# Linear attention, slot mixture and MLP in one kernel: products of the middle chunk with the states placed in the off-diagonal quarters of TensorE, beside the first link of the state chain

## The chip, the cores and the metric

The kernel runs on one core of a Trainium2 chip. The metric is the device time of one execution in microseconds (us), the median of several runs. The engines are TensorE (PE, and PEld for its weight loads), VectorE (DVE), ScalarE (ACT), GpSimd (POOL) and SyncE (SP), whose queue issues nearly all DMAs. Each engine takes its instructions in the order in which they are written; semaphores order them across engines.

## The reference

Three stages follow each other. The first is a gated linear attention over 4 batches, 8 heads, 768 steps and 48 features:

```python
for t in range(S):
    state = alpha[:, :, t, :, None] * state + np.einsum('bhd,bhe->bhde', k[:, :, t], v[:, :, t])
    y[:, :, t] = np.einsum('bhd,bhde->bhe', q[:, :, t], state)
```

The second takes its output as 3072 tokens of 384 features into a soft mixture of 8 experts with 4 slots each: logits `x @ phi`, a softmax over tokens that gathers the slots, two matrix products per expert (`w1`, `w2`), and a softmax over slots that gives them back. The third is a gated MLP (`w_gate`, `w_val`, `w_out`) from 384 over 1536 to 384 features. All is computed to float32 accuracy.

## The kernel before

The attention is worked off in a loop of 32 steps (`fast`, L622). Step g is half a sequence (3 chunks of 128 time steps) of one unit n, that is of two heads s = 0 and 1, which lie on partitions 0 to 47 and 64 to 111. Eight steps are one batch. Within a half, three kinds of product make y:

- S = k^T q per chunk and head (`emit_s`, L353), masked to its triangle by DVE (L360) for head 0, and by an ACT copy (L362) and a POOL select (L363) for head 1; then masked S with v (`emit_ip`, L432);
- the state before the chunk with q (`emit_past`, L420), which all chunks have but the first of a sequence;
- the chain of states: k^T v of each chunk (`emit_dh`, L390), to which a link adds the state before by a product with an identity (`emit_st`, L402); ACT scales the sum into the next state (L404).

A float32 product appears as two MATMUL records. L402 and L420 use 64 rows by 64 columns of the array: head 0 the upper left quarter, head 1 the lower right. L353 uses 64 rows by 128 columns, L390 and L432 128 rows by 64 columns, and the transposes of k (`emit_kt`, L371) and of y (`emit_xt`, L462) and the logits (`emit_l`, L453) have shapes of their own.

The order on every engine is that of the code; the loop is a software pipeline written by hand. Step g issues, for PE: the first link of g, S of g+1, the second link, the transposes of k of g+1 and of x = y of g-1, the logits of g-1, now and then a piece of the softmax slots (`pend`), the past products of g, dh of g+1, and the masked products of g. ACT copies the sum of the past and the masked products to x (L434) at the end of the step. DVE runs the two scans over alpha (L307, L314) for step g+3, POOL scales k and q by them (L325) for step g+2.

Beside this, the MLP's weights are turned to float32: `wgv` comes as 64-bit words in 24 loads of 384 KB, one issued by `pump_gv` at the end of a step into one of two buffers. Each takes an ACT pass (`conv_y`, L249) and three DVE passes (`conv(0)`, `conv(1)`, `conv(2)`: L253, L257, L261), spread over one step. `conv_y` stands in ACT's order right after the first link's ACT work; a condition (L627) keeps it out of steps 0 and 1, and out of two steps of each eight after the first eight.

PSUM: PE's products for kt, dh, xt and the slot pieces come from one rotating pool of three banks (`psm`, L179); y has one bank (`ps_y`), in which a past product opens the accumulation and the masked ones close it.

SP issues per step the loads of v (for g+4), of k and q (for g+5) and of alpha (for g+6) as their buffers come free, then one `wgv` load and by a credit (`RATE`) the blocks of `w1`, `w2` and `wo`. After the loop follow the slot softmax of the last batch, the experts (L856, L914) and, from about 190 us to the end, the MLP (L1010, L1011, L1049).

Of the kernel before, what the change touches and what calls it, by code (L numbers as in the profile page):

```python
# [8 lines left out]
F32 = mybir.dt.float32  # L9
# [9 lines left out]
CH = 128  # L19
# [3 lines left out]
NU = H // 2  # L23
NE, NSL, FE = 8, 32, 1024
# [9 lines left out]
LAST = 4  # L34
GV0, RATE = 1, 840
TINY = 2.0 ** -55
NEAR, ROUND = 31600, 19184
LA = 3
# [54 lines left out]
def attention_slots_mlp(ctx: ExitStack, tc: tile.TileContext, kq, at, vt, phi, w1, w2, wgv, wo, cst, out):  # L93
    nc = tc.nc
# [11 lines left out]
    negm = cs[:, 288:289]  # L106
    phs = const.tile([112, NU, NSL], F32, name="phs")
    tots = const.tile([112, B * NU, NC], F32, name="tots")
# [32 lines left out]
    def program(general):  # L141
# [15 lines left out]

        zn = {nm: [0] * n for nm, n in (("a", 4), ("p", 5), ("v", 4), ("w", 2), ("x", 2))}
        zsize = {"a": HW, "p": HB, "v": 288, "w": HW, "x": 384}
        for z in "a0 a1 p2 a2 p3 v0 w0 a3 p4 v1 w1 p0 v2 p1 v3 x0 x1".split():  # L160
            zn[z[0]][int(z[1])] = ar.alloc(zsize[z[0]], 1)
# [10 lines left out]
        def view(r, rows=128):  # L172
            o = r[0] % FAR
            return (near_t if r[0] < FAR else far_t)[0:rows, o:o + r[1]]
# [3 lines left out]

        def psm():  # L179
            return ps_m.tile([128, 512], F32, tag="m", name="m")  # L180

# [195 lines left out]
        def new_g():  # L377
            ng[0] += 1
            return gsts[:, ng[0] % 7, :]

        def emit_dh(g):
            n, h = sgs[g]
            vv[g] = have.pop(("v", g))
            v = view(vv[g]).rearrange("p (c e) -> p c e", e=96)
            t = ktok.pop(g)
            dps[g] = psm()
            for c in range(nk(g)):
                for s in range(2):
                    m = 64 if s == 0 else 48
                    nc.tensor.matmul(dps[g][64 * s:64 * s + m, c * 48:c * 48 + 48], lhsT=t[:, c, 64 * s:64 * s + m], rhs=v[:, c, 48 * s:48 * s + 48], start=(c == 0), stop=True, skip_group_check=True)  # L390

        dps = {}

# [13 lines left out]

        yps = {}


        def emit_past(g):
            n, h = sgs[g]
            q = view(qp[g], 112)
            yps[g] = ps_y.tile([128, 512], F32, tag="y", name="y")
            for c in range(3):
                cc = 3 * h + c
                o = slice(c * CH, (c + 1) * CH)
                for s in range(2) if cc else ():
                    p = slice(0, 64) if s == 0 else slice(64, 112)
                    nc.tensor.matmul(yps[g][p, o], lhsT=gst[n, cc][p, 0:p.stop - p.start], rhs=q[p, o], start=(cc == max(1, 3 * h)), stop=False, skip_group_check=True)  # L420
            del qp[g]
            release(pair.pop(g), z_p, g + 5)

        def emit_ip(g):
            n, h = sgs[g]
            v = view(vv[g]).rearrange("p (c e) -> p c e", e=96)
            ps = yps[g]
            for c in range(3):
                o = slice(c * CH, (c + 1) * CH)
                for s in range(2):  # L430
                    p = slice(0, 64) if s == 0 else slice(64, 112)
                    nc.tensor.matmul(ps[p, o], lhsT=v[:, c, 48 * s:48 * s + p.stop - p.start], rhs=smk[g, s][:, c], start=False, stop=True, skip_group_check=True)  # L432
            xt[g] = (z_x.pop(0), 384)
            nc.scalar.copy(view(xt[g], 112), ps[0:112, 0:384])  # L434
            del smk[g, 0], smk[g, 1], yps[g]
            release(vv.pop(g), z_v, g + 4)

# [7 lines left out]
        def emit_l(g):  # L445
            n, h = sgs[g]
            b, u = units[n]
            if u == 0 and h == 0:
                lps[b] = ps_l.tile([128, 512], F32, tag="l", name="l")
            x = view(xt[g], 112)  # L450
            for j in range(3):
                t0 = j * CH
                nc.tensor.matmul(lps[b][32 * j:32 * j + 32, CH * h:CH * h + CH], lhsT=phs[:, u, :], rhs=x[:, t0:t0 + CH], start=(u == 0 and h == 0), stop=(u == NU - 1), skip_group_check=True)  # L453

        def emit_xt(g, between=lambda: None):
            n, h = sgs[g]
            b, u = units[n]
            x = view(xt[g], 112)
            ps = psm()
            for c in range(3):  # L460
                t0 = c * CH
                nc.tensor.transpose(ps[:, c * 112:(c + 1) * 112], x[:, t0:t0 + CH], ident[0:112, 0:112])  # L462
            between()
            src = bass.AP(ps.tensor, ps.offset, [list(ps.ap[0]), [112, 3], [64, 2], [1, 48]])
            dst = xtok[:, n % 5, 3 * h:3 * h + 3].rearrange("p c (s e) -> p c s e", s=2)
            nc.scalar.copy(dst, src)

        def slot_steps(b):
# [27 lines left out]
            def e_tok():  # L496
# [4 lines left out]
                nc.vector.tensor_copy(st["et"].rearrange("p r e -> p (r e)"), ps[:, 0:192])  # L501

            def part(between=lambda: None):
                ps = psm()
                o = NU * b % 5
                pieces = [(0, o, min(NU, 5 - o))] + [(5 - o, 0, NU - 5 + o)] * (o > 1)
                for r in range(2):
                    if r:
                        between()
                    for u, p, w in pieces:  # L510
                        for j in range(3):
                            nc.tensor.matmul(ps[32 * j:32 * j + 32, 96 * u:96 * u + 96 * w], lhsT=st["et"][:, r, 32 * j:32 * j + 32], rhs=xtok[:, p:p + w, 3 * r + j, :], start=(r == 0 and u == 0), stop=(r == 1), skip_group_check=True)
                if own:
# [62 lines left out]

        def fast():
            pump_units(4)

# [42 lines left out]
            for g in range(NSG):  # L622
                n, h = sgs[g]
                nxt = g + 1 < NSG

                emit_st(g, 1 - h)
                if GV0 < g and (g <= 8 or g % 8 not in (3, 4)):  # L627
                    conv_y()
                if g + 3 < NSG:
# [21 lines left out]
                if g:  # L651
                    emit_l(g - 1)
                    release(xt.pop(g - 1), z_x, g + 1)
                    p = sgs[g - 1][0]
                    if sgs[g - 1][1] == 1 and units[p][1] == NU - 1:
                        pend += slot_steps(units[p][0])
                        late = True
                        pend.pop(0)()
                if pend and not late:
                    pend.pop(0)()  # L660
                emit_past(g)
                if nxt:
# [14 lines left out]
                while credit[0] > 0:  # L677
                    c = credit[0]
                    pump(1)
                    if credit[0] == c:  # L680
                        break
                pump_units()
            for r in z_t:
                drop(r)
# [448 lines left out]
def _arrays(q, k, v, alpha, moe_phi, moe_w1, moe_w2, moe2_w_gate, moe2_w_val, moe2_w_out):  # L1133
# [16 lines left out]
    vt = c(v.reshape(B, NU, 2, NC, CH, D).transpose(0, 1, 4, 3, 2, 5)).reshape(B, NU, CH, NC * 96)  # L1150
    ph = np.zeros((112, NU, NSL), np.float32)
    pr = moe_phi.reshape(NU, 2, D, NSL)
    for s in range(2):
        ph[64 * s:64 * s + 48] = pr[:, s].transpose(1, 0, 2)
    w1 = moe_w1.reshape(2, 4, 3, 128, 2, 512).transpose(0, 4, 2, 1, 3, 5).reshape(2, 2, 4, 3, 128, 512)
# [31 lines left out]
```

## Time and profile before

| | us |
|---|---|
| median of 3 runs | 388.98 (387.81 to 390.64) |
| the profiled execution, own time | 387.89 |
| its span, first to last instruction | 386.2 |
| PE, DVE, ACT, POOL busy over the span | 368.8, 292.4, 200.8, 102.4 |

The page and the views name a line of the code, an engine, an operation, and its tiles as out<-in. In a timeline row the first number is the start from the span's beginning, the second the length; neighbouring instructions of one kind are merged ("x12"), and the idle time before, with what ended it, stands in brackets. A matmul's record is longer than the time that it holds the array, since records overlap; what a group costs is read from start to start. In a windows row stand, for a stretch, its length, then for each engine its busy time and instructions, TensorE's granted clock, the busy share of the DMA engines and their GB/s.

### The profile page before, as it was taken

The numbers are of one execution on the slowest core, as the hardware profiler recorded it, in microseconds if no ns is written. First come the engines' busy times: TensorE is split into PE (matmuls) and PEld (weight loads), VectorE is DVE, ScalarE is ACT, GpSimd is POOL, SyncE is SP. The second block draws the span as 40 slices with busy tenths as digits, with TensorE's granted clock in tenths as the row PEclk, the third lists the DMA queues.
The fourth block names the chain that finished last, engine by engine and source line by source line (L and its number), as shares of the span: only waits on it lengthen the run. The fifth ranks groups of instructions, "written<-read, shape, count | busy, mean of one in ns | idle before, by whom it ended". The sixth has DMA issues, their size and how long they took to land.

```text
span 386.2 us, 8613 instructions
## 1 busy us (share of the span) xinstructions
PE 368.8 (95%) x3308; PEld 277.0 (72%) x3309; DVE 292.4 (76%) x566; ACT 200.8 (52%) x468; POOL 102.4 (27%) x105
## 2 busy tenths in 40 slices
PE   7799999999999999999899999999999999999992
PEld 3577777776777776433478778888888888888781
DVE  6999899999999973306789977777677867977540
ACT  2366665665567455523467655455445446446441
POOL 3379666795587650011200000000000000000000
PEclk9999999999999999999999999999999999999997
DMA  8999999999899986899900013204204104112002
GB/s 276 354 300 343 374 342 316 321 342 338 281 369 361 304 286 217 345 367 413 351 2 0 3 48 111 68 28 126 74 1 153 50 23 153 38 36 82 3 2 90
DMA packets 28627, 74.25 MB, mean 192 GB/s; under 512 B 3216, under 2 KB 11648, under 8 KB 28576
## 3 DMA queue, kind: packets, MB, share of 16 engines
q1 hardware_dynamic: 28256, 73.27, 53.9%
q8 instruction: 28, 0.46, 0.5%
q10 hardware_dynamic: 272, 0.21, 0.2%
q14 instruction: 23, 0.19, 0.2%
q0 software_dynamic: 48, 0.13, 0.1%
HBM read 68.87 MB, written 4.72 MB: 191 GB/s over the span
## 4 chain that ended last, share of the span: by engine, by line
PE 73%; DVE 6%; DMA 3%; ACT 2%; issue 1%; DVEq 0%; ACTq 0%
PE m L1049 22%; PE acc L1049 11%; PE s L353 4%; PE y L432 4%; PE y L420 4%; PE s L1010 4%; PE s L1011 4%; DMA near<-w 3%; PE s L856 3%; PE m L402 3%; PE m L390 2%; PE m L371 2%; PE l L453 2%; PE m L462 2%; DVE near L1016 2%; DVE rnd L1024 1%
## 5 line engine op out<-in xcount | busy, mean ns | idle before, releaser
L1049 PE MATMUL m<-rnd 128*128 128x512 f32 x432 | 129.3, 389 | 0.0
L1049 PEld LDWEIGHTS m<-rnd 128*128 128x128 f32 x432 | 81.1, 188 | 16.8
L1013 ACT ACTIVATE near<-s 128x512 f32<-128x512 f32 x72 | 43.1, 598 | 79.1 <-PE s L1010 79.1
L1049 PE MATMUL acc<-rnd 128*128 128x512 f32 x216 | 81.1, 392 | 0.8 <-DVE rnd L905 0.8
L325 POOL TENSOR_TENSOR far<-far 112x384 f32<-112x384 f32 x61 | 74.5, 1239 | 9.7 <-DVE far L307 4.7
L1016 DVE TENSOR_TENSOR near<-near,s 128x512 f32<-128x512 f32 x72 | 49.3, 685 | 35.3 <-ACT near L1013 35.3
L1024 DVE TENSOR_TENSOR rnd<-near,rnd 128x512 fp32r<-128x512 f32 x72 | 49.4, 686 | 3.1 <-ACT rnd L1022 3.1
L1049 PEld LDWEIGHTS acc<-rnd 128*128 128x128 f32 x216 | 40.5, 188 | 10.2 <-DVE rnd L905 1.6
L1022 ACT CAST rnd<-near 128x512 fp32r<-128x512 f32 x72 | 44.2, 614 | 0.2 <-DVE near L1016 0.2
L404 ACT ACTIVATE far<-m,tots 112x48 f32<-112x48 f32 x80 | 24.2, 302 | 24.1 <-PE m L402 13.3
L307 DVE TENSOR_TENSOR_SCAN far<-far,r 112x388 f32<-112x388 f32 x32 | 30.8, 961 | 5.8 <-DMA far<-at 3.2
L353 PE MATMUL s<-far 64*128 64x128 f32 x384 | 30.5, 289 | 3.5 <-POOL far L325 3.5
L1120 DVE TENSOR_REDUCE amm<-near 112x1 f32<-112x768 f32 x32 | 30.3, 946 | 3.5 <-DMA near<-at 3.5
L363 POOL TENSOR_SCALAR_AFFINE_SELECT far<-far 128x384 f32<-128x384 f32 x32 | 21.7, 677 | 42.3 <-ACT far L362 42.3
L314 DVE TENSOR_TENSOR_SCAN far<-far,r 112x387 f32<-112x387 f32 x32 | 30.7, 959 | 1.1
L434 ACT COPY far<-y 112x384 f32<-112x384 f32 x32 | 15.3, 479 | 27.7 <-PE y L432 27.7
L353 PEld LDWEIGHTS s<-far 64*128 64x128 f32 x384 | 24.4, 187 | 6.1 <-POOL far L325 4.4
L432 PE MATMUL y<-far 128*48 128x128 f32 (+1 forms) x384 | 28.6, 274 | 0.0
L1010 PE MATMUL s<-rnd 128*128 128x512 f32 x72 | 28.3, 393 | 0.0
L1011 PE MATMUL s<-rnd 128*128 128x512 f32 x72 | 28.2, 391 | 0.0
L257 DVE SCALAR_TENSOR_TENSOR near<-near 128x384 uint32<-128x384 uint32 x36 | 21.3, 593 | 8.5 <-ACT near L249 7.6
L261 DVE SCALAR_TENSOR_TENSOR near<-near 128x384 uint32<-128x384 uint32 x36 | 24.5, 681 | 0.3
(163 smaller groups left out, 489.7 us busy)
## 6 DMA issues: line engine op xcount, KB each, us to landing
near<-w SPq DMA_DIRECT2D x18, 768.0 KB, 7.7
far<-kq SPq DMA_DIRECT2D x32, 384.0 KB, 5.3
far<-w SPq DMA_DIRECT2D x14, 768.0 KB, 5.6
near<-wgv SPq DMA_DIRECT2D x24, 384.0 KB, 5.9
far<-at SPq DMA_DIRECT2D x32, 194.0 KB, 5.2
near<-at SPq DMA_DIRECT2D x16, 339.1 KB, 3.4
far<-vt SPq DMA_DIRECT2D x32, 144.0 KB, 4.7
near<-wo SPq DMA_DIRECT2D x12, 384.0 KB, 7.9
```

The costliest lines, as they stand in the source:

```text
L307: nc.vector.tensor_tensor_scan(w[:, ::-1], a[:, ::-1], rst[:, ::-1], 0.0, ALU.mult, ALU.add)
L314: nc.vector.tensor_tensor_scan(a, a, rst[:, 0:387], 0.0, ALU.mult, ALU.add)
L325: eng.tensor_tensor(out=xv, in0=xv, in1=sv, op=ALU.mult)
L353: nc.tensor.matmul(sps[g][s][:, o:o + CH], lhsT=k[64 * s:64 * s + 64, t0:t0 + CH], rhs=q[64 * s:64 * s + 64, t0:t0 + CH], start=True, stop ...
L432: nc.tensor.matmul(ps[p, o], lhsT=v[:, c, 48 * s:48 * s + p.stop - p.start], rhs=smk[g, s][:, c], start=False, stop=True, skip_group_check ...
L1010: nc.tensor.matmul(pg, lhsT=swk[n][:, 128 * o:128 * o + 128], rhs=ctT[t % 4], start=True, stop=True)
L1011: nc.tensor.matmul(pv, lhsT=swk[n][:, 256 + 128 * o:256 + 128 * o + 128], rhs=ctT[t % 4], start=True, stop=True)
L1013: nc.scalar.activation(sg, pg, AF.Silu)
L1016: nc.vector.tensor_tensor(out=h_, in0=sg, in1=pv, op=ALU.mult)
L1022: nc.scalar.copy(hi, h_)
L1024: nc.vector.tensor_tensor(out=lo, in0=h_, in1=hi, op=ALU.subtract)
L1049: nc.tensor.matmul(p, lhsT=passes[j][0][:, sl], rhs=passes[j][1], start=(f == 0 and j == 0), stop=(f == NF - 1 and j == 2))
```

## The change

The past products of step g-1 move from the end of their step into step g, right behind its first link. The masked products now come first and open the accumulation, the past products close it, and the copy to x moves with them. The middle chunk (c = 1) is computed with its two heads swapped: head 0's columns go to partitions 64 and up and head 1's to 0 to 63, so that its past products use the two other quarters of the array, and it has a PSUM bank of its own. So x is copied in two pieces (128 and 256 columns). What reads x undoes the swap: `phs` is held twice, the second time with the heads exchanged, and the gather of slots reads the middle chunk's columns in the other order (`x_rows`). The three rotating banks are allocated once: bank 0 for dh and the links, bank 1 for the middle chunk, kt and the slot pieces, bank 2 for xt. One of the two x buffers goes, `far` shrinks by 128 columns for the larger `phs`, and `conv_y` starts in step 1 in place of step 2, behind the two copies.

```diff
-GV0, RATE = 1, 840
+RATE = 840
-NEAR, ROUND = 31600, 19184
+NEAR, ROUND = 31600, 19056
...
-    phs = const.tile([112, NU, NSL], F32, name="phs")
+    phs = const.tile([112, 2, NU, NSL], F32, name="phs")
...
-        def psm():
-            return ps_m.tile([128, 512], F32, tag="m", name="m")
+        mb = []
+
+        def psm(i=1):
+            return mb[i] if mb else ps_m.tile([128, 512], F32, tag="m", name="m")
...
-            dps[g] = psm()
+            dps[g] = mb[0]
...
+        def swap(c):
+            return int(c == 1 and not general)
+
+        def half(s):
+            return slice(0, 64) if s == 0 else slice(64, 112)
+
+        def y_out(g, s, c):
+            return yps[g][c == 1][half(s ^ swap(c)), CH * (c // 2):CH * (c // 2) + CH]
+
+        def emit_ip(g):
+            yps[g] = ps_y.tile([128, 512], F32, tag="y", name="y"), mb[1]
+            v = view(vv[g])
+            for c in (0, 2, 1):
+                for s in range(2):
+                    o = y_out(g, s, c)
+                    e = 96 * c + 48 * s
+                    nc.tensor.matmul(o, lhsT=v[:, e:e + o.shape[0]], rhs=smk[g, s][:, c], start=(c < 2), stop=True, skip_group_check=True)
+            del smk[g, 0], smk[g, 1]
+            release(vv.pop(g), z_v, g + 4)
 
         def emit_past(g):
             n, h = sgs[g]
             q = view(qp[g], 112)
-            yps[g] = ps_y.tile([128, 512], F32, tag="y", name="y")
             for c in range(3):
                 cc = 3 * h + c
-                o = slice(c * CH, (c + 1) * CH)
                 for s in range(2) if cc else ():
-                    p = slice(0, 64) if s == 0 else slice(64, 112)
-                    nc.tensor.matmul(yps[g][p, o], lhsT=gst[n, cc][p, 0:p.stop - p.start], rhs=q[p, o], start=(cc == max(1, 3 * h)), stop=False, skip_group_check=True)
+                    o = y_out(g, s, c)
+                    nc.tensor.matmul(o, lhsT=gst[n, cc][half(s), 0:o.shape[0]], rhs=q[half(s), c * CH:(c + 1) * CH], start=False, stop=True, skip_group_check=True)
+            xt[g] = (z_x.pop(0), 384)
+            x = view(xt[g], 112)
+            y, z = yps.pop(g)
+            nc.scalar.copy(x[:, CH:2 * CH], z[0:112, 0:CH])
+            nc.scalar.copy(x.rearrange("p (c t) -> p c t", t=CH)[:, 0::2], y[0:112, 0:2 * CH].rearrange("p (c t) -> p c t", t=CH))
             del qp[g]
             release(pair.pop(g), z_p, g + 5)
...
         def emit_l(g):
...
-                nc.tensor.matmul(lps[b][32 * j:32 * j + 32, CH * h:CH * h + CH], lhsT=phs[:, u, :], rhs=x[:, t0:t0 + CH], start=(u == 0 and h == 0), stop=(u == NU - 1), skip_group_check=True)
+                nc.tensor.matmul(lps[b][32 * j:32 * j + 32, CH * h:CH * h + CH], lhsT=phs[:, swap(j), u, :], rhs=x[:, t0:t0 + CH], start=(u == 0 and h == 0), stop=(u == NU - 1), skip_group_check=True)
...
-            ps = psm()
+            ps = psm(2)
...
                 emit_st(g, 1 - h)
-                if GV0 < g and (g <= 8 or g % 8 not in (3, 4)):
-                    conv_y()
+                if g:
+                    emit_past(g - 1)
+                    if g <= 8 or g % 8 not in (3, 4):
+                        conv_y()
...
-                emit_past(g)
...
+            emit_past(NSG - 1)
+            mb.clear()
```

On PE the place is from the logits of a step over its past products to the next ones. Before, in step 2 (l logits, y past products with the bank's number, m dh):

```order
L453 MATMUL l_266<-far_94,phs_73 32x128 x3
L420 MATMUL y_270<-far_94 64x128
L420 MATMUL y_270<-far_94 48x128
L420 MATMUL y_270<-far_94 64x128
L420 MATMUL y_270<-far_94 48x128
L420 MATMUL y_270<-far_94 64x128
L420 MATMUL y_270<-far_94 48x128
L390 MATMUL m_277<-far_94 64x48
```

Now, at the start of the next step (L405 the link, L441 the past products of the step before, m_96 the middle chunk's bank, L356 the S products):

```order
L405 MATMUL m_95<-far_94,cs_72 64x48
L405 MATMUL m_95<-far_94,cs_72 48x48
L441 MATMUL y_279<-far_94 64x128
L441 MATMUL y_279<-far_94 48x128
L441 MATMUL m_96<-far_94 48x128
L441 MATMUL m_96<-far_94 64x128
L441 MATMUL y_279<-far_94 64x128
L441 MATMUL y_279<-far_94 48x128
L356 MATMUL s_310<-far_94 128x128
```

The six past products left their place between the logits and dh and stand behind the link, the middle pair with its column counts exchanged.

On ACT the place is step 3, from the link's ACT work (L404) to the copy of S. Before, L434 being the copy to x:

```order
L434 COPY far<-y 112x384
L404 ACTIVATE far<-m,tots 112x48
L249 ACTIVATE near<-near 128x384
L404 ACTIVATE far<-m,tots 112x48
L374 COPY far<-m 128x336
L466 COPY far<-m 128x288
L362 COPY far<-s 128x384
```

Now, with the same work under L407, L445 and L446 (the copies to x), L252, L377, L478 and L365:

```order
L407 ACTIVATE far<-m,tots 112x48
L445 COPY far<-m 112x128
L446 COPY far<-y 112x2x128
L252 ACTIVATE near<-near 128x384
L407 ACTIVATE far<-m,tots 112x48
L377 COPY far<-m 128x336
L478 COPY far<-m 128x288
L365 COPY far<-s 128x384
```

The one copy ahead of the link's ACT work became two behind it, still ahead of `conv_y`.

On DVE the place is the work of step 1 (scans of step 4, mask of step 2). Before, up to the next step's start:

```order
L306 MEMSET r 112x4
L307 SCALAR_TENSOR_TENSOR far<-far,r 112x388
L309 TENSOR_TENSOR tots<-far,r 112x3
L310 RECIPROCAL r<-tots 112x3
L314 SCALAR_TENSOR_TENSOR far<-far,r 112x387
L360 TENSOR_TENSOR far<-s,cs 128x384
```

Now, the same step with the first conversion in it (L256, L260, L264):

```order
L309 MEMSET r 112x4
L310 SCALAR_TENSOR_TENSOR far<-far,r 112x388
L256 TENSOR_SCALAR near<-near 128x384
L312 TENSOR_TENSOR tots<-far,r 112x3
L313 RECIPROCAL r<-tots 112x3
L317 SCALAR_TENSOR_TENSOR far<-far,r 112x387
L260 SCALAR_TENSOR_TENSOR near<-near 128x384
L363 TENSOR_TENSOR far<-s,cs 128x384
L264 SCALAR_TENSOR_TENSOR near<-near 128x384
```

Every conversion up to step 10 moved one step ahead. On SP the order of the loads is the same up to there; so a `wgv` load, issued at the end of the same step as before, stands one step nearer to the conversion that reads it. The load of k and q waits for the past products in addition, which free its buffer later than before.

More of the change, by code (lines that the diff above doesn't have):

```diff
@@ L156, in program @@
         z_c = [(ar.alloc(GP, 0), GP)]
-        zn = {nm: [0] * n for nm, n in (("a", 4), ("p", 5), ("v", 4), ("w", 2), ("x", 2))}
+        zn = {nm: [0] * n for nm, n in (("a", 4), ("p", 5), ("v", 4), ("w", 2), ("x", 1))}
         zsize = {"a": HW, "p": HB, "v": 288, "w": HW, "x": 384}
-        for z in "a0 a1 p2 a2 p3 v0 w0 a3 p4 v1 w1 p0 v2 p1 v3 x0 x1".split():
+        for z in "a0 a1 p2 a2 p3 v0 w0 a3 p4 v1 w1 p0 v2 p1 v3 x0".split():
             zn[z[0]][int(z[1])] = ar.alloc(zsize[z[0]], 1)
@@ L379, in new_g @@
             return gsts[:, ng[0] % 7, :]
+        dps, yps = {}, {}
         def emit_dh(g):
@@ L390, in emit_dh @@
                     nc.tensor.matmul(dps[g][64 * s:64 * s + m, c * 48:c * 48 + 48], lhsT=t[:, c, 64 * s:64 * s + m], rhs=v[:, c, 48 * s:48 * s + 48], start=(c == 0), stop=True, skip_group_check=True)
-        dps = {}
         def emit_st(g, c):
@@ L406, in emit_st @@
                 del dps[g]
-        yps = {}
+        def swap(c):
[14 more added lines that the diff above has]
+            release(vv.pop(g), z_v, g + 4)
         def emit_past(g):
@@ L413, in emit_past @@
             q = view(qp[g], 112)
-            yps[g] = ps_y.tile([128, 512], F32, tag="y", name="y")
             for c in range(3):
                 cc = 3 * h + c
-                o = slice(c * CH, (c + 1) * CH)
                 for s in range(2) if cc else ():
-                    p = slice(0, 64) if s == 0 else slice(64, 112)
-                    nc.tensor.matmul(yps[g][p, o], lhsT=gst[n, cc][p, 0:p.stop - p.start], rhs=q[p, o], start=(cc == max(1, 3 * h)), stop=False, skip_group_check=True)
+                    o = y_out(g, s, c)
[5 more added lines that the diff above has]
+            nc.scalar.copy(x.rearrange("p (c t) -> p c t", t=CH)[:, 0::2], y[0:112, 0:2 * CH].rearrange("p (c t) -> p c t", t=CH))
             del qp[g]
             release(pair.pop(g), z_p, g + 5)
[L424 to L436, printed above, removed]
         def release(r, z, g):
@@ L501, in e_tok, with x_rows @@
                 nc.vector.tensor_copy(st["et"].rearrange("p r e -> p (r e)"), ps[:, 0:192])
+            def x_rows(p, w, r, j):
+                x = xtok[:, p:p + w, 3 * r + j, :]
+                if swap(j):
+                    x = bass.AP(x.tensor, x.offset + 48, [list(x.ap[0]), list(x.ap[1]), [-48, 2], [1, 48]])
+                return x
             def part(between=lambda: None):
@@ L511, in part @@
                         for j in range(3):
-                            nc.tensor.matmul(ps[32 * j:32 * j + 32, 96 * u:96 * u + 96 * w], lhsT=st["et"][:, r, 32 * j:32 * j + 32], rhs=xtok[:, p:p + w, 3 * r + j, :], start=(r == 0 and u == 0), stop=(r == 1), skip_group_check=True)
+                            nc.tensor.matmul(ps[32 * j:32 * j + 32, 96 * u:96 * u + 96 * w], lhsT=st["et"][:, r, 32 * j:32 * j + 32], rhs=x_rows(p, w, r, j), start=(r == 0 and u == 0), stop=(r == 1), skip_group_check=True)
                 if own:
@@ L577, in fast @@
         def fast():
+            mb.extend([psm() for _ in range(3)])
             pump_units(4)
@@ L652, in fast @@
                     emit_l(g - 1)
-                    release(xt.pop(g - 1), z_x, g + 1)
+                    release(xt.pop(g - 1), z_x, g)
                     p = sgs[g - 1][0]
@@ L1150, in _arrays @@
     vt = c(v.reshape(B, NU, 2, NC, CH, D).transpose(0, 1, 4, 3, 2, 5)).reshape(B, NU, CH, NC * 96)
-    ph = np.zeros((112, NU, NSL), np.float32)
+    ph = np.zeros((112, 2, NU, NSL), np.float32)
     pr = moe_phi.reshape(NU, 2, D, NSL)
     for s in range(2):
-        ph[64 * s:64 * s + 48] = pr[:, s].transpose(1, 0, 2)
+        for x in range(2):
+            ph[64 * s:64 * s + 48, x] = pr[:, s ^ x].transpose(1, 0, 2)
     w1 = moe_w1.reshape(2, 4, 3, 128, 2, 512).transpose(0, 4, 2, 1, 3, 5).reshape(2, 2, 4, 3, 128, 512)
```

## The prediction

> **What bounds the kernel now.** I read the page first, then the attention loop by windows, then the rows of one pair of steps engine by engine.
>
> ```profile
> span 386.2 us, 8613 instructions
> PE 368.8 (95%) x3308; PEld 277.0 (72%) x3309; DVE 292.4 (76%) x566; ACT 200.8 (52%) x468; POOL 102.4 (27%) x105
> ...
> core 0: us, PE busy (x) PEld busy (x) DVE busy (x) ACT busy (x) POOL busy (x), PEclk, DMA share, GB/s
> 21.34:152.90 131.56, 129.40 (x1950) 99.51 (x1946) 118.37 (x262) 79.78 (x232) 87.97 (x85) 1.00 0.93 323
> 110.00:120.00 10.00, 10.00 (x151) 7.86 (x154) 9.60 (x22) 6.70 (x20) 9.98 (x8) 1.00 1.01 363
> ```
>
> The loop takes up to 152.9 us, and PE has 98% of its main part (129.40 of 131.56). But in ten undisturbed us of it everything is full: PE 10.0, POOL 9.98, DVE 9.6, the DMA engines 1.01. A saving on PE is therefore worth what the others let through. The granted clock is 1.00 throughout, so no cost here is the clock's.
>
> Now PE over an even and an odd step (a step begins with its first L402):
>
> ```profile
> 101.34 0.31 PE L402 MATMUL m<-far,cs 64*64 64x48 f32 x4
> ...
> 105.28 0.31 PE L402 MATMUL m<-far,cs 64*64 64x48 f32 x4
> 105.53 0.94 PE L353 MATMUL s<-far 64*128 64x128 f32 x12
> ...
> 107.36 0.42 PE L453 MATMUL l<-far,phs 112*32 112x128 f32 x6
> 107.71 0.87 PE L420 MATMUL y<-far 64*64 64x128 f32 x12
> 108.51 0.49 PE L390 MATMUL m<-far 128*64 128x48 f32 x11
> ...
> 109.66 0.31 PE L402 MATMUL m<-far,cs 64*64 64x48 f32 x4
> ...
> 111.98 0.65 PE L420 MATMUL y<-far 64*64 64x128 f32 x8
> 112.56 0.43 PE L390 MATMUL m<-far 128*64 128x48 f32 x8
> 112.78 0.44 PE L432 MATMUL y<-far 128*48 128x128 f32 x4
> ```
>
> Two steps take 109.66 - 101.34 = 8.32, so 4.16 each. From start to start the link costs 105.53 - 105.28 = 0.25, six past products 108.51 - 107.71 = 0.80, four 112.56 - 111.98 = 0.58. So a pair on the two diagonal quarters costs 0.22, and a group 0.14 besides (0.80 - 3 x 0.22): the change of the array's shape. The link is 0.14 + 0.11.
>
> **Part 1, PE: past products beside the link.** One group replaces two. Before: 0.25 + 0.80 = 1.05, or 0.25 + 0.58 = 0.83. After, with the middle pair running beside the others: 0.14 + 0.11 + 2 x 0.22 = 0.69, or 0.47. That saves 0.36 either way: 0.14 for one change of shape, 0.22 for the hidden pair. With 30 such groups in steps 2 to 31 this is 30 x 0.36 = 10.8 us. Step 1 gives nothing, since PE waits there for POOL anyway, and the past products of step 31 follow the loop alone. No row shows four quarters at work. Bounds: nothing hidden (0.14 a step, 4.2 in all) and 10.8. I take 10.8, since L453's six records on the same 112 rows, in three sets of columns, cost 107.71 - 107.36 = 0.35, where three products one after the other would cost at least 0.66 at 0.11 a record: sets that share their rows do run together. The order of the masked products (c = 0, 2, 1), `phs` twice and `x_rows` change neither counts nor shapes: 0; the swapped read of x moves the same elements.
>
> The Trainium skill, in "TensorE: Matmul & The Clock Gate", Part 3, "The mechanism", says that a weight load overlaps running products only when their row groups differ. The middle pair shares its row groups with the others, so by that rule it would not be hidden, and the sum would be 4.2 in place of 10.8; the L453 row speaks against it.
>
> **Part 2, the copies of kt.** Past products no longer stand between the logits and dh, and dh reads the ACT copy of kt.
>
> ```profile
> 105.98 0.56 ACT L249 ACTIVATE near<-near 128x384 f32<-128x384 f32 x1
> 106.76 0.30 ACT L404 ACTIVATE far<-m,tots 112x48 f32<-112x48 f32 x1 [0.23 <-PE m L402]
> 107.23 0.44 ACT L374 COPY far<-m 128x336 f32<-128x336 f32 x1 [0.17 <-PE m L371]
> ...
> 150.28 0.31 PE L402 MATMUL m<-far,cs 64*64 64x48 f32 x4 [0.55 <-ACT far L404]
> ```
>
> In the odd step the copy ends at 107.67 and the logits at 107.71, so 0.04 is left. The x copy in two pieces costs one more fixed part on ACT, which waits 0.23 and 0.17 in this stretch: hidden, between 0 and 0.3 a step on dh. I take 0.5 us in all, nearer the low end. Fixed banks: kt in bank 1 has to wait for the copy of the middle chunk, but S (0.86) and a link stand between: 0, up to 0.2 if ACT is late.
>
> **Part 3, DVE and POOL behind PE.**
>
> ```profile
> 107.79 0.54 DVE L360 TENSOR_TENSOR far<-s,cs 128x384 f32<-128x384 f32 x1
> 108.26 0.54 DVE L261 SCALAR_TENSOR_TENSOR near<-near 128x384 uint32<-128x384 uint32 x1
> 108.81 0.06 DVE L306 MEMSET r<- 112x4 f32 x1
> ...
> 111.37 0.53 DVE L257 SCALAR_TENSOR_TENSOR near<-near 128x384 uint32<-128x384 uint32 x1
> 111.82 0.55 DVE L360 TENSOR_TENSOR far<-s,cs 128x384 f32<-128x384 f32 x1
> 112.29 0.80 DVE L261 SCALAR_TENSOR_TENSOR near<-near 128x384 uint32<-128x384 uint32 x1
> ...
> L261 DVE SCALAR_TENSOR_TENSOR near<-near 128x384 uint32<-128x384 uint32 x21 | 16.2, 772 | 0.0
> ...
> 136.12 1.82 POOL L325 TENSOR_TENSOR far<-far 112x384 f32<-112x384 f32 x2
> ...
> 136.34 0.96 DVE L307 TENSOR_TENSOR_SCAN far<-far,r 112x388 f32<-112x388 f32 x1
> ...
> 137.74 0.96 DVE L314 TENSOR_TENSOR_SCAN far<-far,r 112x387 f32<-112x387 f32 x1
> ...
> 145.73 0.94 PE L353 MATMUL s<-far 64*128 64x128 f32 x12
> ...
> 152.11 0.87 PE L432 MATMUL y<-far 128*64 128x128 f32 x12
> ```
>
> DVE does not wait for PE: the mask of step 22 ends at 108.33, L432 reads it at 112.78, 4.45 later, and L360 and L261 start as the one before ends. So a faster PE does not make DVE faster; it eats that lead. If DVE keeps its times, the last scan ends at 138.70, POOL's second product 0.91 later (1.82 for two), and the last S starts at about 139.7 in place of 145.73. From there to the last masked products it is 6.38 now (152.11 - 145.73), less 0.36, less the 0.55 that PE idles at 150.28 and that past products fill: 5.47, so 145.2 in place of 152.11. This limit allows 6.9. The first conversion one step earlier puts one more among the scans: 0.45 for L257 (111.82 - 111.37), 0.55 for L261 (108.81 - 108.26) and a little for L253, 1.1. That leaves 5.8. DVE's own times can move: L261 takes 772 ns on average and 540 where nothing is in its way, so at most 21 x 0.23 = 4.9 come back, and as much may be added.
>
> **Part 4, loads and waits that move.** From step 1 to 10 each `wgv` is converted one step after its load's issue, not two. `conv_y` then waits for the landing, and behind it on ACT stand the second link's scaling and the copy of kt, for which PE waits in dh; on DVE L253 waits too.
>
> ```profile
> 21.09 0.31 PE L402 MATMUL m<-far,cs 64*64 64x48 f32 x4
> ...
> 21.64 0.38 SPq L223 DMA_DIRECT2D far<-kq  x1
> 22.11 0.38 SPq L219 DMA_DIRECT2D far<-at  x1
> 22.60 0.37 SPq L244 DMA_DIRECT2D near<-wgv  x1
> ...
> DMA to landing us min/median/max: 4.3/5.9/8.1
> ...
> 57.99 1.29 PE m L512 x12
> ```
>
> Issue is 1.5 after the step's start (22.60 - 21.09) and landing 4.3 to 8.1 later. The next step starts after 4.16 - 0.36 = 3.8, and ACT reaches `conv_y` some 1.2 into it (0.7 in the rows above, at 105.98, plus the copies). A stall s lengthens the step before too, so s = 1.5 + lat - 3.8 - s - 1.2, that is (lat - 3.5) / 2: 0.4, 1.2 or 2.3 for the three latencies. Longer steps relieve full DMA engines, so I take 0.6, near the low end. Steps 2 to 8 pay: 7 x 0.6 = 4.2. Steps 9 and 10 hold slot products (1.29 in one piece) and are long enough. After the two steps without conversion two loads are ahead again. DVE waits at most as long as ACT, 4.2, and at least 0; I put 0.8, since it has the 4.45 of Part 3 to be late in. The load of k and q is issued 0.55 into the step today (21.64 - 21.09) and now waits for past products that end 0.47 to 0.69 into it: up to 0.2 later, with the alpha and `wgv` loads behind it on SP, which the 0.6 holds already. POOL's order does not change.
>
> **The sum.** PE: -10.8 + 0.5 + 4.2 = -6.1. DVE: -5.8 + 0.8 = -5.0. The smaller gain decides, so -5.0. After the loop nothing changes: the last w2 and wo loads, which fill the DMA engines, start when the experts free their space, and move with PE.
>
> ```profile
> 160.00:190.00 30.00, 28.70 (x291) 11.15 (x291) 12.87 (x29) 10.88 (x25) 6.11 (x6) 1.00 1.00 393
> ```
>
> Against the profiled execution, 387.89 (386.2 and 1.7 around it), this gives 382.9. That run lies 1.1 under the median of 388.98; against the median, 384.0.
>
> **Rivals.**
> 1. PE's whole saving arrives: DVE gets its stretched conversions back and no load is late: 389 - 10.5 = 378.5. For it, the 4.9 in L261; against it, POOL at 9.98 of 10, whose products are what DVE meets. Chance 0.10.
> 2. The middle pair isn't hidden (each weight load waits for the products on its rows): the step shrinks by 0.14. PE: -4.2 + 0.5 + 3.5 (s = 0.5 in seven steps, since they are longer) = -0.2, so 388.8. This is the skill's rule, of which the L453 row shows the contrary. Chance 0.15.
> 3. ACT becomes what PE waits for: 0.3 before each dh, at Part 2's upper end, is 9 us against 10.8, with the stalls shared: about -2, so 387. The copies and `conv_y` stand ahead of kt's; the waits of 0.23 and 0.17 speak against it. Chance 0.14.
> 4. Slower: the `wgv` stall of Part 4 stays at the latency of loaded engines. At 8.1, s = 2.3 in seven steps is 16.1: -10.8 + 0.5 + 16.1 = +5.8, so 394.8. It decides from s = 1.5 (10.3 / 7, a latency of 6.5), and by over 1% from s = 2.0. For it: 1.01 of the DMA engines at today's pace; against: such stalls slow the demand. Chance 0.13.
>
> **How the numbers follow.** The forecast has 0.48, the rivals 0.52. Over 1% (3.9 us, about what a measurement tells from no change) faster: the forecast's part that passes 3.9, 0.43, rival 1 with 0.10 and a rest of 0.01: 0.54. Slower by over 1%: 0.11 of rival 4. Within 1%: 0.35. The range starts at 379.5 (DVE gets back most of its stretch) and ends at 390.5 (rivals 2, 3 and the mild part of 4): outside lie about 0.08 below and 0.12 above.
>
> **What would show it.** Link and past products together take 0.47 and 0.69 from start to start (Part 1); 0.69 and 0.91 mean rival 2. dh starts right behind the logits, with no wait for kt's copy over 0.1. In steps 2 to 8 ACT waits at `conv_y` for `wgv`, in later ones not. The time from mask to masked products falls from 4.45 to under 2. I am wrong if DVE begins to wait for PE, or if PE waits for POOL's scaled k and q in most steps.

## The result and the profile after

The changed kernel takes 393.15 us in the median of 20 runs (389.8 to 398.1), the kernel before 388.49 in 20 runs beside it (386.83 to 390.71). The ratio is 1.0102, with an interval of 1.0073 to 1.0131: about 1% slower, where 384.0, faster than before, was forecast. Medians here are over all runs, and ratios leave disturbed runs out, so a ratio can lie nearer to 1 than the quotient of its medians. The profiled execution took 392.8, with a span of 391.0, which is 4.8 more than before.

The page of the changed kernel: the span, the busy engines, and the granted clock in 40 slices of 9.8 us.

```profile
span 391.0 us, 8743 instructions
PE 363.8 (93%) x3309; PEld 269.7 (69%) x3309; DVE 290.0 (74%) x566; ACT 203.4 (52%) x500; POOL 102.6 (26%) x105
...
PEclk8989999999999999999999999999999999999997
```

PE has 5.0 us less to do (363.8 in place of 368.8) and the kernel is still longer. So it is waits that grew. To place them, take the starts of S, by half (the halves of a sequence are numbered as the steps; S of half i is issued in step i-1):

| start of S, half | before | after | difference | what lies between |
|---|---|---|---|---|
| 3 | 21.34 | 20.86 | -0.48 | |
| 11 | 55.83 | 61.33 | +5.50 | 5.98 lost in 8 steps |
| 13 | 65.75 | 71.85 | +6.10 | 0.60 lost |
| 31 | 145.73 | 151.14 | +5.41 | 0.69 gained in 18 steps |
| end of the span | 386.2 | 391.0 | +4.8 | |

Two things need explaining: the 6 us lost by half 11, and why the 18 steps behind half 13 gain only 0.7.

**Steps 2 to 9.** The waits of the changed kernel from 20 to 62 us: engine, line and what it waited for, then the sum, how often, the longest.

```profile
ACT near L252 <- DMA near<-wgv: 8.8, 6, 2.2
...
DVE near L256 <- DMA near<-wgv: 5.6, 5, 1.7
PE m L395 <- ACT far L377: 5.2, 4, 1.6
```

ACT waits for `wgv` in `conv_y` (L252), DVE in the first part of its conversion (L256), and PE in dh (L395) for the copy of kt (L377). One step shows how they hang together, from the timelines of SP, DVE, ACT and PE around step 2 (in brackets the idle time before, and what ended it):

```profile
18.32 0.43 SPq L247 DMA_DIRECT2D near<-wgv  x1
...
23.48 0.36 DVE L256 TENSOR_SCALAR near<-near 128x384 uint32<-128x384 uint32 x1 [1.71 <-DMA near<-wgv]
...
21.04 0.37 ACT L446 COPY far<-y 112x256 f32<-112x256 f32 x1
23.56 0.55 ACT L252 ACTIVATE near<-near 128x384 f32<-128x384 f32 x1 [2.15 <-DMA near<-wgv]
24.02 0.28 ACT L407 ACTIVATE far<-m,tots 112x48 f32<-112x48 f32 x1
24.21 0.33 ACT L377 COPY far<-m 128x224 f32<-128x224 f32 x1
...
22.60 0.42 PE L465 MATMUL l<-far,phs 112*32 112x128 f32 x6
24.59 0.48 PE L395 MATMUL m<-far 128*64 128x48 f32 x8 [1.57 <-ACT far L377]
```

The load was issued at 18.32 and let ACT and DVE go at about 23.5, 5.2 later; with one step of lead ACT stood at it from 21.41. Behind it in ACT's order stand the second link's scaling and the copy of kt, so dh starts 1.57 late. After this wait the clock dropped too; after the three others at dh (1.23, 1.01 and 1.41) it did not. The changed kernel by windows (length; PE, PEld, DVE, ACT, POOL busy; granted clock; DMA share; GB/s), three short stretches and the eight steps:

```profile
22.00:24.60 2.60, 1.03 (x15) 0.62 (x13) 1.05 (x4) 1.04 (x4) 0.34 (x1) 1.00 0.88 333
24.60:28.10 3.50, 3.50 (x40) 2.84 (x42) 2.93 (x6) 1.50 (x5) 2.81 (x3) 0.53 0.90 333
28.10:31.50 3.40, 3.40 (x64) 2.70 (x60) 3.03 (x8) 2.29 (x7) 1.03 (x3) 0.98 0.86 267
...
20.86:61.33 40.47, 33.44 (x513) 25.40 (x511) 33.59 (x74) 22.46 (x72) 24.74 (x26) 0.96 0.94 323
```

The second row, 3.5 us at a clock of 0.53, costs 3.5 x 0.47 = 1.6 us. So the stretch adds up: eight steps should have gained 8 x 0.34 = 2.7 and lost 5.98, together 8.7. Of it 5.2 are waits for the copy of kt, 1.6 the clock, and 1.8 four waits in step 9, a slot step (0.50, 0.31, 0.20 and 0.79 in PE's timeline): 8.6. The kernel before waited 0.45 in step 9 itself, so the account leaves about half a microsecond open.

**Steps 13 to 30.** The steps between slot steps are as fast as hoped: S follows S by 3.60 and 4.05 in place of 3.94 and 4.37. But two whole batches, 16 steps, take the same time. The windows of before, then of after, from half 14 to half 30:

```profile
69.69:141.36 71.67, 70.51 (x1077) 54.50 (x1073) 68.14 (x153) 43.17 (x127) 50.20 (x49) 1.00 0.94 329
```

```profile
75.44:147.09 71.65, 67.11 (x1074) 49.78 (x1072) 67.16 (x154) 44.33 (x143) 53.99 (x49) 1.00 0.95 331
```

PE is busy 3.4 less, and the length is the same to 0.02. The missing time sits in the slot steps. After's timelines of DVE, ACT and PE around step 17:

```profile
91.36 0.42 DVE L493 TENSOR_TENSOR nmx<-nmx 96x1 f32<-96x1 f32 x1
...
91.88 0.47 ACT L500 ACTIVATE e<-l,nmx 96x256 f32<-96x256 f32 x1 [2.10 <-DVE nmx L493]
...
92.78 0.30 ACT L407 ACTIVATE far<-m,tots 112x48 f32<-112x48 f32 x1
...
91.35 1.01 PE L356 MATMUL s<-far 64*128 64x128 f32 x12 [0.55 <-POOL far L328]
93.13 0.31 PE L405 MATMUL m<-far,cs 64*64 64x48 f32 x4 [0.77 <-ACT far L407]
...
96.13 0.44 PE L430 MATMUL m<-far 128*48 128x128 f32 x4 [0.28 <-DVE e L513]
```

PE is ahead of DVE by then. DVE finds the logits' peak (L493) after the mask, ACT waits 2.10 for it with its exponent (L500), and the first link's scaling (L407) stands behind that; PE waits in the link. It waits as well for POOL's scaled k and q, and for DVE's reading of a bank that the middle chunk needs. Before, ACT came to the exponent of this step without a wait.

Of the two batches the first gains 0.55 (35.84 to 35.29, halves 14 to 22) and the second gives 0.53 back (35.83 to 36.36). In the second a `wgv` load came late once more, in step 24, and PE waited in dh:

```profile
124.23 0.55 ACT L252 ACTIVATE near<-near 128x384 f32<-128x384 f32 x1 [1.26 <-DMA near<-wgv]
...
125.26 0.43 PE L395 MATMUL m<-far 128*64 128x48 f32 x8 [0.69 <-ACT far L377]
```

### The profile page after: what moved, and what is told of

Same layout as the page of the kernel before. It is cut to its first block, busy times and chain, and to the rows that moved or that the text cites. A ratio compares the mean times of both kernels' runs of the same rounds, so it can differ in the third digit from the quotient of the medians.

```text
span 391.0 us, 8743 instructions
## 1 busy us (share of the span) xinstructions
PE 363.8 (93%) x3309; PEld 269.7 (69%) x3309; DVE 290.0 (74%) x566; ACT 203.4 (52%) x500; POOL 102.6 (26%) x105
## 4 chain that ended last, share of the span: by engine, by line
PE 52%; DVE 8%; ACT 2%; issue 1%; DVEq 0%; ACTq 0%
PE m L1072 22%; PE acc L1072 11%; PE s L1033 4%; PE s L1034 4%; PE s L879 3%; PE so L937 2%; DVE near L1039 1%; DVE rnd L1047 1%; PE sw L1002 1%; DVE near L793 1%; DVE rnd L928 1%; DVE near L264 1%; PE s L356 1%; PE s L853 1%; PE y L430 1%
## 5 line engine op out<-in xcount | busy, mean ns | idle before, releaser
L407 ACT ACTIVATE far<-m,tots 112x48 f32<-112x48 f32 x80 | 23.9, 299 | 36.6 <-PE m L405 33.8
L356 PE MATMUL s<-far 64*128 64x128 f32 x384 | 31.2, 292 | 3.7 <-DVE r L309 1.9
L356 PEld LDWEIGHTS s<-far 64*128 64x128 f32 x384 | 25.1, 191 | 9.8 <-issue 4.2
L252 ACT ACTIVATE near<-near 128x384 f32<-128x384 f32 x36 | 20.2, 565 | 12.3 <-DMA near<-wgv 11.2
L260 DVE SCALAR_TENSOR_TENSOR near<-near 128x384 uint32<-128x384 uint32 x36 | 19.8, 550 | 7.5 <-ACT near L252 6.6
L256 DVE TENSOR_SCALAR near<-near 128x384 uint32<-128x384 uint32 x36 | 13.6, 377 | 15.4 <-DMA near<-wo 9.2
L264 DVE SCALAR_TENSOR_TENSOR near<-near 128x384 uint32<-128x384 uint32 x36 | 23.4, 650 | 0.3
## 6 DMA issues: line engine op xcount, KB each, us to landing
far<-kq SPq DMA_DIRECT2D x32, 384.0 KB, 5.1
near<-wgv SPq DMA_DIRECT2D x24, 384.0 KB, 5.5
near<-wo SPq DMA_DIRECT2D x12, 384.0 KB, 8.9
```

The lines of the kernel that those rows point to most:

```text
L356: nc.tensor.matmul(sps[g][s][:, o:o + CH], lhsT=k[64 * s:64 * s + 64, t0:t0 + CH], rhs=q[64 * s:64 * s + 64, t0:t0 + CH], start=True, stop ...
```

## The experiments

Theory A: the load's lead, one step short, costs the 6 us, and for the rest the loop is held by DVE, which has no gap, so that PE's saving pays little. B: the loop is PE's once the late loads are gone. C: the banks, the quarters or the two copies cost the time. D, A1, A2, K and E are told where they come up.

| kernel | median, us | ratio to before, interval |
|---|---|---|
| after, conversions from step 2 (E1) | 386.08 | 0.9953, 0.9926 to 0.9980 |
| before, conversions from step 1 (E2) | 397.42 | 1.0128, 1.0044 to 1.0212 |
| E1 on the diagonal quarters (E3) | 389.21 | 1.0033, 1.0014 to 1.0052 |
| E1, DVE lighter (E4) | 381.97 | 0.9846, 0.9801 to 0.9891 |
| before, DVE lighter (E5) | 389.37 | 1.0014, 0.9982 to 1.0046 |
| E1, slot results in bank 2 (E6) | 387.93 | 0.9983, 0.9951 to 1.0014 |
| E1, exponent later (E7) | 387.48 | 0.9966, 0.9933 to 0.9998 |
| E1, both of these (E8) | 384.73 | 0.9907, 0.9877 to 0.9936 |
| after, ACT's conversion later (E9) | 398.23 | 1.0235, 1.0202 to 1.0268 |
| after, PE filled (E10) | 395.25 | 1.0158, 1.0120 to 1.0196 |
| E4 on the diagonal quarters (E11) | 384.80 | 0.9897, 0.9860 to 0.9933 |
| after, two loads in step 0 (E12) | 386.85 | 0.9947, 0.9915 to 0.9980 |

The kernel before, run beside them, had medians of 388.0 (with E1, E2, E4, E5), 388.22 (E3, E6 to E8), 388.71 (E9 to E11) and 389.06 (E12).

**E1, the old lead given back.**

```diff
-                    if g <= 8 or g % 8 not in (3, 4):
+                    if g > 1 and (g <= 8 or g % 8 not in (3, 4)):
                         conv_y()
```

> The changed kernel, with the conversions of wgv begun in step 2 as before, so that each load has two steps to land. Theory A (the conversion one step early makes ACT wait for wgv, and PE behind it; for the rest VectorE, which has no gap, sets the loop's pace): ACT's waits for wgv in steps 2 to 10 fall from 8.8 us to under 1, the granted clock comes back to 0.993, and the time is 386 to 388, that is 0.5 to 2.5 under the kernel before and 5 to 7 under the changed kernel, since VectorE's order is that of before and only the tail after its last scan shrinks. Theory B (the loop is TensorE's once the waits are gone): 0.33 us in each of 30 steps arrive, 378 to 381. Theory C (the loss comes from the fixed banks, the quarters or the two copies of x): 391 to 394, as with the change whole.

386.08: what A said, 1.9 under before and some 7 under the change; B's 378 to 381 and C's 391 are out. No wait for `wgv` is left among the waits from 20 to 62 us, and from half 3 to half 11 it takes 33.87 (20.81 to 54.68), where the change takes 40.47 and the kernel before 34.49. So the 6 us came back where they had been lost. The clock did not come back, though: 0.983 in the profiled run. Windows of E1 around step 17, a slot step, show why:

```profile
82.00:86.00 4.00, 2.52 (x46) 1.95 (x45) 3.87 (x8) 1.69 (x8) 3.70 (x4) 1.00 1.02 347
86.10:92.90 6.80, 6.80 (x66) 5.17 (x66) 6.40 (x15) 3.67 (x11) 2.62 (x3) 0.50 0.73 263
```

PE idled 1.5 of 4 us (the waits of the slot step), then ran 6.8 us at half clock: 3.4 us, more than the waits themselves.

**E2, the short lead alone.**

```diff
-GV0, RATE = 1, 840
+GV0, RATE = 0, 840
```

> The kernel before, with only the conversions of wgv begun in step 1; quarters, banks and the order of the past products as before. Theory A: ACT waits for wgv by 1 to 2 us in most of steps 2 to 8, the time is 392 to 396, and the clock drops in places. Theory B says the same of this run. Theory C: no more than 1 us over the kernel before, 388 to 390.

The median, 397.42, lies over A's 392 to 396, but the six runs spread from 390.12 to 401.02, and the ratio rests on two of them (390.12 and 395.75). So the kernel before is slower with the short lead alone, without quarters, banks or copies; by how much stays open between 0.4 and 2.1%. The waits of the profiled run (397.67) from 20 to 62 us (lines as before):

```profile
ACT near L249 <- DMA near<-wgv: 8.7, 6, 2.0
...
DVE near L253 <- DMA near<-wgv: 4.3, 4, 2.0
```

The loads are not all of its loss, though. By half 11 this run is 6.05 behind the kernel before, and 3.0 of that is step 1 alone (7.48 from S to S in place of 4.46). There PE waited 2.23 for POOL, as in the kernel before (2.22), and ran at a clock of 0.54 behind it. The two steps by windows, before and E2:

```profile
16.88:21.34 4.46, 4.46 (x69) 3.55 (x69) 4.17 (x10) 1.84 (x6) 1.91 (x3) 1.00 0.95 330
```

```profile
16.70:24.20 7.50, 7.46 (x68) 5.97 (x68) 6.97 (x15) 1.92 (x6) 2.91 (x4) 0.54 0.66 240
```

**E12, the lead without the later start.**

```diff
                 pump_gv()
+                if g == 0:
+                    pump_gv()
```

> The changed kernel with one line more: step 0 issues two wgv loads in place of one, so that each load has two steps to land though the conversions begin in step 1 as in the change. Theory A2 (what costs is the lead of one step alone): the time is that of the kernel with conversions from step 2, 385 to 388, with under 1 us of waiting for wgv after step 2. Rival E (the conversion's work for VectorE and ACT among the first, short steps is itself part of the loss, or the second early load delays k, q and alpha when the DMA engines are full at 10 to 16 us): 389 to 392.

386.85, the time of E1, with the conversions in step 1 as in the change. Here too no wait for `wgv` is among those of 20 to 62 us, and halves 3 to 11 take 33.77. E falls: neither the conversion's early work nor the second load costs anything that shows. Two different edits that give the lead back, E1 and E12, both bring the time back; the lead is the cause.

**E9, whose wait it is.** ACT's part moves behind the copy of x; a stand-in lets DVE's parts keep their places.

```diff
-                conv(1)
                 if nxt:
...
                 if g:
                     emit_xt(g - 1)
+                conv_y_late()
+                conv(1)
                 if nxt:
                     emit_masks(g + 1)
```

> The changed kernel, conversions still from step 1, but ACT's part of the conversion stands behind the link's scaling, the copy of kt and the copy of x, in place of ahead of them; VectorE's three parts keep their places. Theory A1 (TensorE loses the time because the copy of kt and the link's scaling stand behind ACT's wait for wgv): TensorE's waits for the copy of kt fall from 5.2 us to under 1.5 in steps 2 to 10 and the time comes near the kernel with conversions from step 2: 385.5 to 388.5. Theory A2 (VectorE's own wait for wgv, 5.6 us, and behind it the masks, hold the loop as much): the waits move to the masked products and to the scaled k and q, and the time stays at 390.5 or more.

398.23, worse than the change, so the time that A1 forecast did not come. The waits of E9 from 16 to 62 us (its lines stand 5 further down: L361 is S, L368 DVE's mask, L410 the link, L412 its scaling):

```profile
DVE near L256 <- DMA near<-wgv: 3.4, 3, 2.2
...
PE m L410 <- ACT far L412: 2.0, 2, 1.5
...
PE s L361 <- DVE far L368: 1.5, 4, 0.5
```

PE's wait for the copy of kt fell from 5.2 to 0.5, as A1 said (its weight loads wait for it by 2.2), and halves 3 to 11 still take 40.83 (the change: 40.47). PE now waits for DVE's masks, which stand behind DVE's own wait. But the experiment is not clean: ACT's later conversion holds up DVE in all later steps too, by 8.3 us from 62 to 160 us (L260 waiting for L252). It shows that taking the wait from ACT alone does not help; how the two engines' waits share the loss, it leaves open.

**E4 and E5, DVE lighter.** In both, the third DVE part of each `wgv` conversion is left out.

```diff
-                to_f32_s(dst, gvy.pop(i))
+                del gvy[i]
```

> The kernel with conversions from step 2, and without the third VectorE operation of each wgv conversion (the sign bits are left out, so the experts' gate and value weights are not the reference's): 24 operations of 0.55 to 0.8 us less on VectorE, all else as it was. Theory A (VectorE sets the pace of the loop behind TensorE's new speed): 6 to 10 us less than with conversions from step 2, so 377 to 381; steps of 3.60 and 4.05 throughout and the logits' exponent no longer waits for VectorE. Theory B (TensorE sets the pace): within 1.5 us of the kernel with conversions from step 2.

> The kernel before, also without the third VectorE operation of each wgv conversion (sign bits left out). Theory A: TensorE is 98% busy there, so the time falls by 3 us at most (385.5 to 388.5): the two engines bound the loop together, and only both savings together pay. If VectorE alone had bounded the kernel before, it falls by 6 or more, to 382.

On the new order it brings 386.08 - 381.97 = 4.1 us, on the old one nothing (389.37 beside 388.0). E5 by windows, over the loop:

```profile
21.34:152.90 131.56, 129.19 (x1948) 99.15 (x1948) 105.94 (x237) 80.21 (x233) 77.41 (x85) 1.00 0.92 328
```

DVE has 12 us less than before there (105.94, was 118.37), PE is as full as ever. So PE holds the kernel before, with DVE close behind: relieving DVE alone brings 0, PE alone 1.9 (E1), both 6.0 (E4). A said 6 to 10 for E4, B at most 1.5; A's direction holds, its size was too large.

**E3 and E11, the quarters.** The middle chunk goes back to the diagonal quarters, in its own bank.

```diff
-            return int(c == 1 and not general)
+            return 0
```

> The kernel with conversions from step 2, but with the middle chunk's products on the same two diagonal quarters as the others (its own bank stays). Link and past products together take 0.69 and 0.91 us from start to start in place of 0.47 and 0.69, so TensorE gets 30 x 0.22 = 6.6 us more to do. Theory A (VectorE paces the loop, so only part of TensorE's saving arrives): 1 to 3 us above the kernel with conversions from step 2, that is 387 to 389, about the kernel before. Theory B (TensorE paces it): 5.5 to 7 above, 391.5 to 393. That the other quarters hide nothing: the same time and the same 0.47 and 0.69.

> The kernel with conversions from step 2 and without the third VectorE operation of each wgv conversion (sign bits left out), with the middle chunk on the same diagonal quarters as the others. Theory A (TensorE's saving is worth its full size once VectorE has room): 5 to 7 us over the same kernel with the other quarters, 387 to 389. If TensorE was not the bound even there: less than 3 us over it, under 385.

PE's timeline, an odd and an even step (link, then S), first E3, then the change:

```profile
72.99 0.31 PE L405 MATMUL m<-far,cs 64*64 64x48 f32 x4
...
73.90 0.94 PE L356 MATMUL s<-far 64*128 64x128 f32 x12
...
77.02 0.31 PE L405 MATMUL m<-far,cs 64*64 64x48 f32 x4
...
77.72 0.94 PE L356 MATMUL s<-far 64*128 64x128 f32 x12
```

```profile
106.44 0.25 PE L405 MATMUL m<-far,cs 64*64 64x48 f32 x2
...
107.13 0.94 PE L356 MATMUL s<-far 64*128 64x128 f32 x12
...
110.25 0.25 PE L405 MATMUL m<-far,cs 64*64 64x48 f32 x2
...
110.73 0.94 PE L356 MATMUL s<-far 64*128 64x128 f32 x12
```

From link to S it is 0.91 and 0.70 on the diagonal, 0.69 and 0.48 with the other quarters: the middle pair is hidden, 0.22 a step, 6.6 us of PE's work in 30 steps. In time that is worth 389.21 - 386.08 = 3.1 (A: 1 to 3; B: 5.5 to 7), and with DVE lighter 384.80 - 381.97 = 2.8 (2.0 by the ratios, which set each beside its own runs of the kernel before), where A had said 5 to 7. So A is not the whole of it: with DVE relieved, something else takes more than half of PE's saving. The E4 kernel still waits in slot steps, and by windows it has such a stretch of low clock around step 25, which the fuller PE of E11 has not (its slices of the clock are all at 9 up to the last):

```profile
117.00:120.00 3.00, 1.77 (x19) 1.13 (x19) 2.84 (x8) 2.97 (x12) 0.78 (x1) 1.00 1.03 390
120.00:123.00 3.00, 3.00 (x41) 2.56 (x40) 2.83 (x9) 0.95 (x4) 2.53 (x3) 0.53 0.94 350
```

**E6, E7 and E8, the slot steps.** D: what remains of the saving is lost where the slot steps tie ACT and PE to DVE. E6 gives the slot pieces bank 2 (the first lines of the diff, alike in `part` and `l_tok`); E7 puts the exponent behind the link's scaling and the copies of x (the others); E8 does both.

```diff
         def e_tok():
-                ps = psm()
+                ps = psm(2)
...
                 if g:
                     emit_past(g - 1)
+                    if late:
+                        pend.pop(0)()
+                        pend.pop(0)()
...
-                if late:
-                    pend.pop(0)()
-                    pend.pop(0)()
```

> The kernel with conversions from step 2, with the slot products' three small results (exponents' transposes, partial sums, logits' transposes) in the third fixed bank, that of x's transposes, in place of the second, which the middle chunk's masked products need right after. Removes TensorE's waits of 0.3 to 0.8 us for VectorE's reading of that bank in the slot steps, four batches of them. If these waits are on the path: 1 to 3 us less than with conversions from step 2. Theory A (VectorE paces these steps anyway): within 0.7 us.

> The kernel with conversions from step 2, with the exponent of the slot logits and the copy of the logits put behind the first link's scaling and the two copies of x on ACT, so that ACT no longer waits 2.3 us for the logits' peak with the link's scaling behind it. Theory D (what is left of TensorE's saving is lost where the slot steps tie ACT and TensorE to VectorE, and the clock halves after those gaps): TensorE's waits of 1.0 to 1.2 us at the link go, the granted clock returns to 0.993, and the time falls by 2 to 4 us, to 382 to 384. Theory A in its strict form (VectorE has no gap and paces everything): within 1 us, 385 to 387.

> The kernel with conversions from step 2, with both edits: slot products in the third bank, and the exponent behind the link's scaling. Theory D: the sum of the two, 3 to 5 us less than with conversions from step 2, 381 to 383; strict theory A: within 1.5 us.

Alone, neither helps: 387.93 and 387.48, no better than E1. In E7 PE's waits in the link, 2.2 us in E1 from 20 to 150 us, are gone, but its waits for DVE's reading of the bank rise from 0.8 to 2.8. Together they reach 384.73, which beats both kernels of the case, by 0.9% under before (the interval ends at 0.9936). D expected 381 to 383, so it holds in part at most, and since E1's interval (0.9926 to 0.9980) touches E8's, that the two edits add to E1 is not settled. In E8 ACT's waits of 62 to 150 us for the peak are 1.2 us in all, in E1 4.7:

```profile
ACT e L500 <- DVE nmx L493: 1.2, 2, 0.7
```

```profile
ACT e L500 <- DVE nmx L493: 4.7, 2, 2.4
```

But in E8 PE waits in the slot transposes for the copy of x in bank 2 instead (1.6 us in two waits). A part of the wait was moved.

**E10, the clock.** K: 2 to 3 us of the loss are the halved clock.

```diff
                 if nxt:
+                    if 2 <= g <= 10:
+                        keep_warm(4)
                     emit_dh(g + 1)
```

> The changed kernel with four idle products of 512 columns (about 0.22 us each, nothing reads them) ahead of dh in steps 2 to 10, where TensorE waits for the copy of kt. They add work to TensorE and shorten no other engine's. Theory K (a good part of the loss, 2 to 3 us, is the clock, which the gate halves after a stretch with TensorE half idle): the mean granted clock rises from 0.981 to 0.988 or more and the time falls to 390 to 392. If the lower clock costs nothing beside the waits: 393 to 396, since the steps without a wait get up to 0.9 us longer.

395.25: not K's 390 to 392, but within the 393 to 396 of a clock that costs nothing beside the waits. Still it doesn't decide between them. The profiled run has the full clock from 16 to 60 us, so the filling does what it should; but it costs 0.97 us in each of nine steps, also in those without a wait, and the loads come late all the same. From half 2 to half 11 this kernel takes 48.1, the change 44.6: of 8.7 us of filling 5.2 were made up for, by waits that it filled and by the clock, which this run does not tell apart. A price of the clock can't be read from it; that stays a reading of the traces.

## Why the prediction was wrong

The forecast took -5.0, with PE at -6.1 and DVE at -5.0; it was +4.7 between the medians.

- **Part 1 held.** 0.47 and 0.69 from link to S were forecast, 0.48 and 0.69 measured. A step shrank by 0.34 and 0.32, where 0.36 was put. The rule of the Trainium skill ("TensorE: Matmul & The Clock Gate", Part 3, "The mechanism"), that a weight load overlaps running products only in other row groups, would have given 0.91 and 0.69, which E3 shows on the diagonal; with quarters that share their rows the pair is hidden all the same.
- **Part 2 held.** Where no load was late, dh starts behind the logits (88.88 to 89.22 in PE's timeline) without a wait. E1 has one exception, 0.63 in step 24, behind a conversion that ACT began 1.20 late, probably for a load as well: the slowest landed 8.2 after its issue.
- **Part 4 failed most: the mechanism was there, the size was not.** In the sum that decided, -5.8 + 0.8 for DVE, the late loads stood with 0.8; they cost 393.15 - 386.08 = 7.1. "I take 0.6, near the low end": ACT waited 2.15, 0.79, 1.80, 1.65, 0, 2.06 and 0.35 in steps 2 to 8, 1.26 on average, which is about what the prediction's own formula gives for the median landing time (1.2). On PE 5.2 arrived at dh, near the 4.2 that were put there; but the same late loads also stopped DVE for 5.6 ("I put 0.8, since it has the 4.45 of Part 3 to be late in"), and behind one of the waits the clock was halved, 1.6. How ACT's and DVE's waits share the 7.1 stays open (E9). "Steps 9 and 10 ... are long enough" did not hold either: ACT waited 1.18 in step 10, and 1.26 in step 24. So rival 4 came true in its direction. That its 394.8 lies near 393.15 is partly luck: it put 2.3 a step where 1.26 came, and a saving of 10.3 where 1.9 arrived.
- **Part 3 failed too.** "So a faster PE does not make DVE faster; it eats that lead." It hardly ate any of it: the lead from a mask to its masked products fell from 4.45 to 3.66 (113.43 to 117.09), not under 2. With the late loads of the first steps gone (E1, E12) the change is worth 1.9 and 2.2 us, not the 5.8 of that limit. In the changed kernel 18 steps brought 0.69 in place of 18 x 0.34 = 6.1. The traces place the loss in the slot steps, where ACT, and behind it PE, wait for DVE once a batch; that DVE holds the loop there is shown by E4 (4.1 us), but that this one wait is what costs is not shown, since E7 takes PE's wait in the link away and gains nothing by itself. What the fixed banks, the two copies and the single x buffer take of the saving no run shows apart.
- "The granted clock is 1.00 throughout, so no cost here is the clock's": true of before, and taken over to a kernel in which PE has waits.

## What to carry to other kernels

When a pipeline step is moved, count the lead of every load that hangs on it in steps and compare it with the landing time under load, for each engine that reads the load: here one condition lost a step of lead, which cost about 7 us, and a second load at the start (E12) or the old condition (E1) gave it back. Where a second engine is nearly as full, a saving on the first is worth little until the second is relieved: here 1.9 us, and 6.0 with both. A wait on TensorE can cost more than itself, since the clock behind it may be halved: in E1 3.4 us behind 1.5 of waiting.

## What the hardware showed that was not expected

The half clock came after short waits. The change's stretch of 3.5 us at 0.53 followed 2.6 us with PE busy for 1.03, whose longest wait was 1.57; E1's 6.8 us at 0.50 followed 4 us with PE busy for 2.52 and waits of 0.45 and 1.03. The Trainium skill ("TensorE: Matmul & The Clock Gate", Part 1, "What's actually happening") puts the half clock after at least one idle window of about 3.4 us, in a window that runs free of the kernel. The traces agree on the half and on the lengths, about one and two such windows; they differ in that no idle time of 3.4 us stood ahead. Nor does the length of a wait decide it: behind the 2.2 us for POOL in step 1 the kernel before kept the full clock, and the profiled run of E2 had 0.54 over 7.5 us. What decides it, no run here shows.

It also shows from run to run: of the 20 runs of the change, the three with a mean clock of 0.993 to 0.995 took 389.8 to 390.3 us, and the two at 0.976 and 0.977 took 395.4 and 395.2. That is a correlation within one kernel, and E10 did not turn it into a price. The 23 runs of the kernel before beside E1 had 0.986 to 0.998.
